# Token weights loaded in 9216-byte runs and turned as fp32 products with the identity, the first queries too

## The chip, the core and the metric

The kernel runs on one core of a Trainium2 chip. The metric is the device time of the program in microseconds (us). TensorE (PE) multiplies, VectorE (DVE), ScalarE (ACT) and GpSimd (POOL) do the rest, SyncE (SP) and ACT issue the transfers (DMA).

## The reference

Eight batches, eight heads, 576 tokens, head size 64, all fp32. Linear attention with a norm, then a block that mixes tokens and channels:

```python
kv  = einsum('bhsd,bhse->bhde', k, v)
out = einsum('bhsd,bhde->bhse', q, kv)
x   = out / sqrt(mean(out*out, -1) + 1e-6) * g_norm      # then heads side by side: (8, 576, 512)
theta = x @ w_theta
zr, zi = x * cos(theta), x * sin(theta)
u = x + einsum('ts,bsd->btd', w_tok_r, zr) + einsum('ts,bsd->btd', w_tok_i, zi)
result = u + maximum(u @ w_ch, 0)
```

The token weights w_tok_r and w_tok_i are 576 x 576. The mix contracts over s, so PE needs them with s on the partitions; in memory they lie with t as rows. They must be turned once.

## The kernel before

**Tiling.** The 576 tokens of a batch are cut into four tiles of 128 rows and one of 64 tokens, whose two halves of 256 columns share the 128 partitions (`full(j)` tells them apart). Token g*9 + r lies at place r*64 + g, so that a partition reads long runs from memory.

**A batch** is: kv (L262, fp32 products of 64 x 64 in four quarters of the array, two calls of 36), its copy to the block matrix kbd (L278), turning of q (L293, or by a transposing transfer from batch 2 on, L301), raw = q kv (L332), square and sum (L355, L365), the root on POOL (L371), x (L380), turn of x (L403), theta (L444), the sine and cosine (L449 to L491; abs, L468, is on ACT or DVE), z (L493, in zm and zt; on DVE or POOL), the token mix (L510), u (L528), turn of u (L536), channel mix (L546), gain (L551), the last sum (L561), store (L576).

**The first stage**, which the change touches: q, k and v of batch 0 and the weights come in by loads on the two queues of SP and ACT. The fp32 token weights land in the buffers that K and V of batch 1 use later (`wtok_s`, L201), the rows of the last 64 places in `wtail_s` (L202). Each matrix comes as two half loads of 64 partitions, in runs of 2304 bytes, and a tail (L229). `cast_token` (L236) makes fp16 of them in `wn` and `wnt`, ten casts on DVE, ACT and POOL. `w_turn` (L591) turns the casts with ten fp16 transposes for each of nine pieces (four and one for each half of the partitions), and `w_out` (L602) copies 576 columns to `wT`. The fp32 queries of batch 0 and all later ones land in `q_s`, which shares memory with `wn` (L204), are cast (L223) and turned (L293). `idle` (L605) runs products whose result nobody reads.

**The order** is written out by hand: the code after L611 makes a list of tasks with engine, cost and what each needs; `TURNS` (L35 to L98) gives the order in which the tasks are issued, the PSUM bank of each (`@3`) and the engine where it isn't the first choice (`:A`, `:D`, `:G`); `~28` is 28 idle products. The costs in the task list play no part when the kernel runs. Each engine works through its own instructions strictly in that order. Transfers share eight completion counters in turn: a load that reuses a counter is issued only when the load before it on that counter has landed. `tok_ready` (L692) holds the casts, `w_turns` (L752) the turns of the weights; K and V of batch 1 wait for the casts (L719, L721), q of batch 1 for all turns (L753).

Of the kernel before, what the change touches and what calls it, by code (L numbers as in the profile page):

```python
# [35 lines left out]
0 2 3 23 12 6 52 24 9 17 13 25 14 7 10 8 39 4 11 26:A 33 15:G 16:D 53 20 5 27:G 18 ~28@0 117@0 110@1  # L36
21 111:A 131@2 124@3 118:A 132:D 138@4 29 19 28 22 104@5 36 40 125:D 37 46 106:A 105 34 139 112@7
119@1 113 38 120 114 35 107@2 121 115 30 45:D 109:A 108:D 31 49 126@0 122 116 140@5 127 133@6 32 134
128 50 43:A 129 135 47 41:A 123 141 51 44:D 42 136 130 48 92 ~8@2 71@4 248 60 145@2 93 62:A 154@3
61:D 67@7 59:G 142 72:A 75@1 94 146:D 68:A 143 155:D 147@0 137 58:A 95 156@4 144 148 56 57 249 55  # L40
63@2 54 157 172@3 149 250 79@7 76:A 158 69@6 88 181@5 251 150 73@0 160 173:D 163@1 159:A 65@4 89
164:D 161 77@3 64 174@1 151 81 90 162 152 66:D 165@2 91 175 153 96 80:A 182:D 200@4 82 166:D 78 70
221@5 167 83 176 183@7 169 84 168 233@3 74 184:D 259@1 170 185 85 186 178 177 212@6 171 260 97 187
188 201 179 190 98 222 244 180 99 189 261 86 87:A 245 234 262 252 246 264@0 263:A 191@7 265 247
271@1 235 202 253 266@2 203 213 267 254 272:D 292@0 214 268 293 255 273@4 236 413@0 269 274 215 256
402 275 101 294@3 403 414 192 276 295 270 193 404 296 100:D 223 194 405 102:G 257:A 278@6 415 224
258 279 418 237@2 416 417:D 285@7 280@5 297 286 216@6 277 281 287@0 419 103:D 308@1 228 288 299@7
195@4 420 300:D 217 282 301@7 309 421 406 289 283 310@6 196:D 298 407 302:D 311 290 303 408 312 305
422@1 436@4 409 284 225@3 550 218@7 219 423 226:D 551 291 437 314 1 424 326@6 410 317@5 304:A 335@3
327:D 438 306 328@0 552 427 240 313 336 307 227@6 315 425 553 220 318 337@3 229 428 204@7 316 319@5  # L50
412 205 429 329:D 238 197@6 398 430 426 320 411 239@7 330 399 579 366@2 321 332 198 400 322 354@1
323 338:D 241 331:A 580 439 431@0 199 206@5 432 401 339 324 433 441@7 375@6 333 581 325 434 345@3
442 440 582 558 367 341 443 340:A 342 346 207 435 559 344 451@4 460@0 444 452 376 334 560 461 343
453@4 554 561 462@0 445 454 555 208 377 455 562 347 463:D 469@7 556 570 368 378 470 478@5 457 348
557 446@4 565@6 456:A 464 447 571 369 563 458 471@3 566 479:D 466 572 230 448 459 480@0 564 573 472
209 465:A 379@2 231 387@5 467 380:D 449 567 473 710 232 481 468 352 474:A 210 355 450 568 482 569
349@2 211 373 370@3 475 574@4 371:D 356 575 711 350:D 583@6 576 372@7 584 712 357 483:A 577 487@0
351@3 713 585 484 488 593@2 485 714 353 588@1 388 586 589 578 389 731 489@0 594 590 717@3 490 374
382 476 732 491 527@7 587 718 715:A 591 733 390 518@0 477 734 612@6 706 486 381@5 613 722 361 707
592 493 519 492:A 494 708 528 496 358@6 614@1 723 359:D 595 719 709 615 495 596 383 724 598@6 721  # L60
520 616 725 854 716 529 597 720 855 618 521 735@5 603@1 599 497@3 394 736 862 856 600 621@4 604 737
525 360@2 857 622:D 726@0 530 630@1 738 727 623@4 863 631:D 617:A 728 605@7 619 864 362 601 498
624:D 363 606 865 740@1 625 729 632@2 866 607 384 499 608 609 364 620:G 522@4 610 500 506@7 365
626:A 730 507 523 385 602 745@3 739 531@0 741 501@6 386 524@4 867 858 611 532 742 859 508 627 526
743 1024 628 670@5 860 509 633 764@0 649@4 765:D 746 861 634 639@7 502 534 533@0 640:D 636 744 1025
641@2 868 629 750@6 1026 539@7 751 642:D 540 635:A 747 541 1027 702 671 643 748 542 1033 703 645
1019@1 535 637 752 704 644:A 646 513 755@7 1020 766@0 647 756 1034 749 504 757@7 705 767 648 658@3
768 753 1035 1021 758:D 769:A 1036 638 510@0 759 883 1023 672 1022 760 773@7 511:D 761 1028@1 774:D
782@2 884 1029 650 673 770 1037@0 885 1030 503@7 762 754 1031 886 1038 659 505 771 874 1047@5 1039
660 1032 674@6 1040 651 875 661 1042@7 512@1 783:D 876 536 1043 763:G 1048 1041 869@2 877 1044 537  # L70
1012 652 775@0 870 772 538 1045 784@4 675:D 776 1013 1049 679@6 777 1014 1050 871 1046 778:A 1015
514 779 791@0 872 873:D 680 677 1016 780 1051 681 1008 785:D 1057 781:G 887@7 653@1 1009 682 888
878@2 676@3 879 786 1058 792 683@5 889 662@6 793@4 654:D 890 1010 801@0 794 663 795 822@1 1059 880
797 787:A 823 686 678 1011 1074 684 802 796:A 881 798 892@4 685@6 788 800 1075 789 799 810@3 893 656
1076 515 790 897@5 1017:A 811 687 812 546 882 516 1004 1067@6 894 898 1005 891 1060@2 1068 813 517
895 391@7 803 1069 1006 907 824 392:D 1071 1061:D 1052@3 665 1007 1070 691@6 899 692 693 1062 908
1077@7 900 694 1063:A 896 909 1084@2 1064 804 1072 1018 655@6 1159 825 1065 901 805@4 1053 1154@0
1073:G 1085 1066 1160 1078 1086 831@5 1161 1155 1079 1087:A 917@2 1162 1054 806:D 1081 1055 657 924
910@7 1080:A 1082 1156 911:D 1088 1083:G 925 1056 1089 918:D 902@4 393@6 926 1158 912 832 1157 919
903 1168 814@3 913:A 1090:G 1163@7 1110@0 1164 833 921 1165 1169 920:A 664@1 395 1170 1091 922 815:D  # L80
1166 904 934@2 914 834 1171 915 688 666 826@6 1177@3 1092 927@5 827 817 923 667 1167 689 1122@1 928
905 543@6 935 1123 929 690 544 808 1172@7 936 843@5 668 1173 1093@6 937:A 1174 844 669 930:A 845
1094:D 1175 807@2 1178 906 846 931 941 1179 835@4 1111 836 809 916:G 816@5 1176 942 1095 1131@4 1192
1096 1097 818 1182@2 1098 1101@7 1180 1099 938 1193 1102 1100 939 1132 1183 1194 829 1112 932 1103
1113 850 695@6 972@5 1184 1114 696 838 1104 1124 1181 951@0 1105 1115 1185 1125 828@6 933 819 1106
1133 830 940:G 837@7 1186 1126 820 952 821 396 545@3 1117 943@1 1127 547 1187@6 839 1202@2 1188 944
397 1134 1108 960@3 1209 945 1189 947 1107@7 698 946:A 948 1210 961 1190 950 981@4 1109 1211 1116@1
1191 1203:D 1226 847@7 973 1118 1195@6 949 1129 242 1227 1204 962 1196 1138 1135 953 243 1206 1197
1205:A 982 954 1198:A 840 1136 974 963 1207 983 975 1199 1208:G 841 1212@1 1200 976 842 848 1219@2
# [32 lines left out]
def kernel(  # L122
# [844 lines left out]
```

## Time and profile before

| what | value |
|---|---|
| median of 3 runs | 237.19 us (235.02 to 238.41) |
| the profiled execution's own time | 236.83 us |
| its span | 235.1 us |
| busy: PE, DVE, ACT, POOL | 208.4, 181.9, 127.3, 147.1 us |
| chain that ended last: PE, DVE, DMA | 33%, 31%, 15% |
| mean granted clock of TensorE | 0.951 |
| moved by DMA | 49.41 MB, mean 210 GB/s |

The page gives times from the start of the span. L12 is line 12 of the kernel. PE is TensorE at products, PEld its weight loads. A timeline row reads: start, busy time, engine, line, operation, out<-in, shape, count, and in brackets the idle time before it and what ended it. A row of the chain reads: start, length, engine or transfer, out (or line), count. An fp32 product written once in the code shows as two records.

### The profile page before, as it was taken

The page shows a single profiled execution, that of the slowest core. Times are in us where ns is not written, and L with a number is a line of the kernel's source. Part 1 is how long each engine was busy: PE and PEld are TensorE (multiplying, and loading weights), DVE is VectorE, ACT ScalarE, POOL GpSimd, SP SyncE. Part 2 cuts the span into 40 slices and gives each one's busy share as a digit, 9 for nine tenths or more (in the row PEclk, how much of TensorE's full clock was granted, in tenths as well). Part 3 has the DMA queues.
Part 4 walks back from the last instruction along what each step waited for, and adds up shares of the span by engine and source line. Part 5 has one row for each costly group of instructions (what it writes and reads, how often), then busy time and mean ns, then how long its engine had stood idle before and what let it go on. Part 6 is the DMA issues. An engine that isn't in the chain of part 4 may idle for free.

```text
span 235.1 us, 6095 instructions
## 1 busy us (share of the span) xinstructions
PE 208.4 (89%) x2488; PEld 119.7 (51%) x2488; DVE 181.9 (77%) x340; ACT 127.3 (54%) x242; POOL 147.1 (63%) x114
## 2 busy tenths in 40 slices
PE   7866799997779799999897999989799999999971
PEld 2355358564634356655453556545455454564530
DVE  1124755857699998989998989799989978699570
ACT  3033466854775759947485636846796512840100
POOL 3205920027699666769868099978599987566750
PEclk9965559999999999999999999999999999999997
DMA  5999897799798999758999997874543367755676
GB/s 177 347 246 279 190 344 266 219 368 355 179 231 259 360 348 280 95 196 301 287 216 151 211 255 191 263 216 84 98 110 84 65 143 85 165 138 104 168 188 146
DMA packets 47627, 49.41 MB, mean 210 GB/s; under 512 B 28016, under 2 KB 29040, under 8 KB 47600
## 3 DMA queue, kind: packets, MB, share of 16 engines
q1 hardware_dynamic: 38688, 29.53, 54.5%
q10 hardware_dynamic: 8912, 19.50, 25.6%
q8 instruction: 19, 0.31, 0.6%
q14 instruction: 8, 0.07, 0.2%
HBM read 33.10 MB, written 9.44 MB: 181 GB/s over the span
## 4 chain that ended last, share of the span: by engine, by line
PE 33%; DVE 31%; DMA 15%; ACT 9%; issue 4%; SPq 3%; POOL 1%; ACTq 0%; DVEq 0%; POOLq 0%
PE psum L434 10%; PE psum L520 8%; DMA vt<-in_moe_w_tok_i_dram 5%; DVE arg L462 5%; DMA vt<-in_v_dram 5%; PE psum L271 4%; DVE ot L570 4%; DMA kt<-in_k_dram 4%; DVE x L387 4%; PE psum L287 3%; DVE zt L505 3%; DVE zm L497 3%; DVE ss L368 3%; DVE arg L473 3%; PE psum L597 2%
## 5 line engine op out<-in xcount | busy, mean ns | idle before, releaser
L375 POOL TENSOR_TENSOR rt<-ss,mhalf 128x8 f32<-128x8 f32 (+1 forms) x40 | 62.2, 1562 | 43.1 <-DVE ss L368 43.1
L520 PE MATMUL psum<-zm,wT 128*128 128x512 f16 x256 | 67.0, 379 | 1.8 <-DVE zm L497 1.0
L554 POOL TENSOR_TENSOR ug<-u,g 128x512 f32<-128x512 f16 (+1 forms) x40 | 44.1, 1114 | 8.2 <-DVE ot L570 8.1
L520 PEld LDWEIGHTS <-wT 128*128 128x128 f16 x288 | 26.2, 98 | 31.0 <-issue 5.3
L434 PE MATMUL psum<-wth,xT 128*128 128x512 f16 x128 | 32.4, 392 | 2.0 <-DVE arg L462 1.3
L434 PE MATMUL psum<-wch,uT 128*128 128x512 f16 x128 | 32.5, 379 | 1.6 <-DVE uT L319 0.8
L481 ACT ACTIVATE sc<-arg 128x512 f16<-128x512 f32 (+1 forms) x40 | 23.1, 583 | 12.2 <-DVE arg L462 12.2
L570 DVE SCALAR_TENSOR_TENSOR ot<-psum,ug 128x512 f32<-128x512 f32 (+1 forms) x40 | 24.7, 631 | 6.5 <-PE psum L439 3.5
L488 ACT ACTIVATE sc<-arg,quarter 128x512 f16<-128x512 f32 (+1 forms) x40 | 26.6, 673 | 4.0 <-DVE arg L473 3.5
L462 DVE SCALAR_TENSOR_TENSOR arg<-pt,psum 128x512 f32<-128x512 f32 (+1 forms) x40 | 24.4, 626 | 4.8 <-ACT pt L453 4.6
L497 POOL TENSOR_TENSOR zm<-x,sc 128x1024 f16<-128x1024 f16 x11 | 23.8, 2175 | 6.3 <-ACT sc L488 6.3
L271 PE MATMUL psum<-vt,kt 64*64 64x64 f32 x1152 | 22.5, 232 | 5.7 <-DMA vt<-in_v_dram 3.0
L319 POOL CAST qh<-wn 128x1152 f16<-128x1152 f32 (+1 forms) x12 | 12.9, 1087 | 23.3 <-DMA wn<-in_q_dram 23.3
L531 DVE TENSOR_TENSOR u<-psum,x 128x512 f16<-128x512 f32 (+1 forms) x40 | 24.4, 628 | 3.5 <-PE psum L520 3.5
L271 PEld LDWEIGHTS psum<-vt,kt 64*64 64x64 f32 x1152 | 20.3, 145 | 10.1 <-issue 4.5
L368 DVE TENSOR_REDUCE ss<-sqb 128x8 f32<-128x520 f32 x32 | 21.8, 686 | 3.9 <-ACT sqb L359 3.6
L359 ACT ACTIVATE sqb<-psum 128x512 f32<-128x512 f32 x32 | 18.5, 593 | 9.5 <-PE psum L345 9.2
L387 DVE TENSOR_TENSOR x<-psum,rt 128x512 f16<-128x512 f32 x32 | 21.9, 683 | 1.0 <-POOL rt L375 0.9
L453 ACT ACTIVATE pt<-psum 128x512 f32<-128x512 f32 (+1 forms) x25 | 13.7, 560 | 15.9 <-PE psum L434 12.5
L434 PEld LDWEIGHTS <-xT 128*128 128x128 f16 x128 | 11.8, 100 | 16.2 <-issue 3.8
L497 DVE TENSOR_TENSOR zm<-x,sc 128x1024 f16<-128x1024 f16 x21 | 19.9, 951 | 0.1
L471 ACT ACTIVATE arg<-arg 128x512 f32<-128x512 f32 (+1 forms) x27 | 15.5, 581 | 7.0 <-DVE arg L462 7.0
(77 smaller groups left out, 271.3 us busy)
## 6 DMA issues: line engine op xcount, KB each, us to landing
vt<-in_v_dram ACTq DMA_DIRECT2D x7, 1152.0 KB, 7.1
kt<-in_k_dram ACTq DMA_DIRECT2D x7, 1152.0 KB, 6.2
wn<-in_q_dram SPq DMA_DIRECT2D x14, 576.0 KB, 6.8
out_dram<-ot SPq DMA_DIRECT2D x28, 256.0 KB, 3.6
kt<-in_k_dram SPq DMA_DIRECT2D x2, 576.0 KB, 9.9
vt<-in_v_dram ACTq DMA_DIRECT2D x2, 576.0 KB, 10.7
zm<-in_moe_w_theta_dram SPq DMA_DIRECT2D x1, 1024.0 KB, 15.8
zm<-in_moe_w_ch_dram SPq DMA_DIRECT2D x1, 1024.0 KB, 9.3
```

Source lines behind the costliest of these rows:

```text
L271: nc.tensor.matmul(kv_ps[b, lo][at:at + D, i, m - lo, :], kt[b % NKV][rows, hp, j * D:(j + 1) * D], vt[b % NKV][rows, hp, j * D:(j + 1) * ...
L368: nc.vector.reduce_sum(out=ss[:], in_=sq_sb.pop((b, j))[:], axis=AXX)
L375: nc.gpsimd.tensor_tensor(out=rt[:], in0=ss[:], in1=mhalf[:, 0:h], op=ALU.pow)
L387: nc.vector.tensor_tensor(out=x_pair[b, p][:, :, a * HC:(a + 1) * HC].rearrange("p t (h e) -> p t h e", e=D), in0=r[:].rearrange("p (t h e ...
L434: nc.tensor.matmul(t[:], lhs[:, kc, :], w[:, kc, :], start=first, stop=last)
L462: nc.vector.scalar_tensor_tensor(out=arg[:, 0, :], in0=pt_sb.pop((b, j))[:], scalar=MAGIC, in1=th_ps.pop((b, j))[:], op0=ALU.subtract, op1 ...
L488: nc.scalar.activation(out=sc_sb[b, j][:, 1, :], in_=arg_sb.pop((b, j))[:, 1, :], func=AFT.Sin, bias=quarter[:], scale=-TURN * SHRINK,)
L497: e.tensor_tensor(out=zm[b % NZ][:, j, :, :], in0=x.unsqueeze(1).broadcast_to((P, 2, C)), in1=sc[:], op=ALU.mult,)
L520: nc.tensor.matmul(t[:], wT[:, w, j * P:(j + 1) * P], r, start=first, stop=last)
L531: nc.vector.tensor_tensor(out=u[:], in0=y_ps.pop((b, j))[:], in1=x_sb.pop((b, j)), op=ALU.add)
L554: nc.gpsimd.tensor_tensor(out=ug[:].rearrange("p (h e) -> p h e", h=h), in0=u_sb[b, j][:].rearrange("p (h e) -> p h e", h=h), in1=g8[:].un ...
L570: nc.vector.scalar_tensor_tensor(out=ot, in0=v_ps.pop((b, j))[:], scalar=0.0, in1=ug_sb.pop((b, j))[:], op0=ALU.max, op1=ALU.add,)
```

## The change

- `load_token` is one load for each matrix, 128 partitions with one run of 9216 bytes each (w_tok_i on SP, w_tok_r on ACT); the tail is a load of its own. Partition 2g + o now holds rows 4o to 4o + 3 of group g.
- The casts of the token weights are gone, and `wn` and `wnt` with them. `turn_f` turns fp32 data by an ordinary product with an fp32 identity (`ident_f`, a new copy on DVE). `w_turn` does four such products for each half of the partitions, 128 columns each, written to PSUM in the order that `wT` needs; `w_out` copies 512 columns and casts. The tails are turned and copied by two tasks of their own.
- The queries of batch 0 aren't cast either: `q_turn` turns them from `q_s`, eight products of 128 columns a block, alternating between the two halves of the partitions. `q_s` has memory of its own.
- K and V of batch 1 wait for the turns of the weights; q of batch 1 waits only for the turned queries of batch 0.
- `TURNS` is new from end to end. On PE the first stage now has 38, 4, 4, 4, 3, 9 and 9 idle products (28 and 8 before), the first token pieces come in one block of three, the theta products come after all nine pieces. Over the whole program abs moves from ACT to DVE nine times, and zm from DVE to POOL four times, three of them in batch 0.

The diff, without `TURNS` and the costs of tasks:

```diff
@@ -179,13 +178,13 @@
-    wn = const.tile([P, NJ, 2 * S], FP16, name="wn")
-    wnt = const.tile([P, 2, S], FP16, name="wnt")
+    q_s = const.tile([P, NHP, TJ * D], FP32, name="q_s")
+    ident_f = const.tile([P, P], FP32, name="ident_f")
@@ -201,8 +200,6 @@
-    q_s = wn[:].rearrange("p j s -> p (j s)").bitcast(FP32).rearrange("p (n e) -> p n e", n=NHP)
     def load_pairs(eng, dst, src, b, ns):
@@ -226,19 +223,15 @@
-    def load_token(eng, i, o):
+    def load_token(eng, i):
-        if o < 2:
-            eng.dma_start(out=wtok_s[i][o * TL:(o + 1) * TL, :, :], in_=w_in[:, o:TJ - 1:2, :])
-        else:
-            eng.dma_start(out=wtail_s[:, i, :], in_=w_in[:, TJ - 1, :])
-    def cast_token(i, j):
-        if full(j):
-            dst, src = wn[:, j, i * S:(i + 1) * S], wtok_s[i][:, j, :]
-        else:
-            dst, src = wnt[0:TL, i, :], wtail_s[:, i, :]
-        copy_out(dst, src)
+        eng.dma_start(
+            out=wtok_s[i].rearrange("p j s -> p (j s)"),
+            in_=w_in[:, 0:TJ - 1, :].rearrange("g (o j) s -> g o (j s)", o=2))
+    def load_token_tail(eng, i):
+        w_in = (moe_w_tok_r, moe_w_tok_i)[i].rearrange("(g r) s -> g r s", r=TJ)
+        eng.dma_start(out=wtail_s[:, i, :], in_=w_in[:, TJ - 1, :])
     def scale_g():
@@ -290,7 +283,22 @@
+    def turn_f(dst, src, n=P):
+        rhs = ident_f[0:n, 0:n]
+        if len(dst.shape) == 3:
+            rhs = rhs.rearrange("p (g o) -> p g o", o=2)
+        nc.tensor.matmul(dst, src, rhs, start=True, stop=True)
     def q_turn(b, j):
+        if b == 0:
+            p, a = divmod(j, 2)
+            blocks = [(a, NJ * p + m) for m in range(HH)] if full(j) else [(m, TJ - 1) for m in range(2)]
+            t = bank(len(blocks) * P).rearrange("p (m e) -> p m e", e=P)
+            for m, (a, r) in enumerate(blocks):
+                for n in range(2):
+                    turn_f(t[n * D:(n + 1) * D, m, :], q_s[:, 2 * a + n, r * D:(r + 1) * D])
+            tr_ps["q", b, j] = t
+            return
@@ -588,19 +596,31 @@
     def prep(dst, src, kc, by):
+    def w_part(n, o):
+        return (1 - n % 2, n // 2 * 2 + o) if n < 2 * NJ else (o, TJ - 1)
     def w_turn(n):
-        t = psum[:, now[-1].bank, :].bitcast(FP16)[:, 0:NT * P]
+        t = bank()
-            rows = slice(o * TL, (o + 1) * TL)
-            i, r = (1 - n % 2, n // 2 * 2 + o) if n < 2 * NJ else (o, TJ - 1)
+            i, r = w_part(n, o)
+            to = t[o * TL:(o + 1) * TL, :].rearrange("p (o j g) -> p j g o", o=2, j=NJ)
-                nc.tensor.transpose(
-                    t[rows, jj * P:(jj + 1) * P], wn[:, jj, i * S + r:(i + 1) * S:TJ], ident[:])
-            nc.tensor.transpose(t[rows, SM:SM + P], wnt[:, i, r::TJ], ident[:])
+                turn_f(to[:, jj, :, :], wtok_s[i][:, jj, r::TJ])
     def w_out(n):
-        copy_out(wT[:, n, :], tr_ps.pop(("w", n))[:, 0:S])
+        copy_out(wT[:, n, 0:SM], tr_ps.pop(("w", n)))
+    def w_tail_turn(ns):
+        t = bank(len(ns) * TL).rearrange("p (n g) -> p n g", g=TL)
+        for n in ns:
+            for o in range(2):
+                i, r = w_part(n, o)
+                turn_f(t[o * TL:(o + 1) * TL, n - ns[0], :], wtail_s[:, i, r::TJ], TL)
+        tr_ps["wtail", ns[0]] = t
+    def w_tail_out(ns):
+        copy_out(wT[:, ns[0]:ns[-1] + 1, SM:], tr_ps.pop(("wtail", ns[0])))
     def idle(n):
@@ -678,9 +698,7 @@
     def load_q0(a):
-        q_got[0, a] = [add("qc", e, {"ACT": 0.63, "DVE": 0.66}[e],
-                           lambda n=n: cast_q(0, slice(n, n + 1)), [h], -45, alts=cast_alts(TJ * D))
-                       for n, e in ((2 * a, "DVE"), (2 * a + 1, "ACT"))]
+        q_got[0, a] = [h]
@@ -689,18 +707,14 @@
-    tok_ready = {0: [], 1: []}
+    tok_got, tail_got = {}, {}
-        h = []
-        for o, queue in enumerate(("SP", "ACT", "SP")):
-            eng = nc.sync if queue == "SP" else nc.scalar
-            h.append(load(queue, 0.62, 1.55 if o < 2 else 0.5, lambda i=i, o=o, eng=eng: load_token(eng, i, o),
-                          [sp if queue == "SP" else act], -42 - i + 0.1 * o,
-                          16 if o < 2 else 4, 2.8)[1])
-        for j, e in enumerate(("DVE", "ACT", "POOL", "ACT" if i else "DVE", "POOL")):
-            tok_ready[i].append(add("tc", e, {"DVE": 0.5, "ACT": 0.63, "POOL": 0.72}[e],
-                                    lambda i=i, j=j: cast_token(i, j), (h[0:2] if full(j) else h[2:]) + q_got[0, 0] + q_got[0, 1], -41,
-                                    alts=(("DVE", 0.5), ("ACT", 0.63), ("POOL", 0.72))))
+        queue = "SP" if i else "ACT"
+        eng = nc.sync if i else nc.scalar
+        hold = sp if i else act
+        tok_got[i] = load(queue, 0.5, 3.4, lambda i=i, eng=eng: load_token(eng, i), [hold], -42 - i, 32, 2.8)[1]
+        tail_got[i] = load(queue, 0.5, 0.5, lambda i=i, eng=eng: load_token_tail(eng, i), [hold], -41.5 - i, 4,
+                           2.8)[1]
     def load_next_q(b, was, pos):
@@ -717,11 +731,11 @@
-                         old + (tok_ready[0] if b == 1 else []), at - 0.5)
+                         old + (w_turns if b == 1 else []), at - 0.5)
-                         old + (tok_ready[1] if b == 1 else []), at)
+                         old + ([w_turns[n] for n in (0, 2, 4, 6, 8)] if b == 1 else []), at)
-            _, got["wch"] = load("SP", 0.5, 2.7, load_wch, [sp, *tok_ready[0]], -37, 32)
+            _, got["wch"] = load("SP", 0.5, 2.7, load_wch, [sp], -37, 32)
@@ -734,24 +748,28 @@
-    w_ready = []
-    def w_all():
-        turns = []
-        for n in range(2 * NJ + 1):
-            t1 = add("wt", "PE", 0.36, lambda n=n: w_turn(n),
-                     tok_ready[1] * (1 - n % 2) + tok_ready[0] * (n % 2 or n == 2 * NJ), n * 0.1, [PS], shape=1)
-            e = "ACT" if n % 2 else "DVE"
-            t2 = add("wo", e, 0.52 if e == "ACT" else 0.37, lambda n=n: w_out(n), [t1], n * 0.1,
-                     alts=(("DVE", 0.37) if e == "ACT" else ("ACT", 0.52),))
-            t1.readers = [t2]
-            w_ready.append(t2)
-            turns.append(t1)
-        return turns
-    w_turns = w_all()
-    load_next_q(1, w_turns, -36)
+    w_turns, w_ready, w_tails = [], [], []
+    for n in range(2 * NJ + 1):
+        t1 = add("wt", "PE", 0.55, lambda n=n: w_turn(n),
+                 [tok_got[i] for i in (0, 1) if n == 2 * NJ or i != n % 2], n * 0.1, [PS], shape=1)
+        e = "ACT" if n % 2 else "DVE"
+        t2 = add("wo", e, 0.52 if e == "ACT" else 0.6, lambda n=n: w_out(n), [t1], n * 0.1,
+                 alts=(("DVE", 0.6) if e == "ACT" else ("ACT", 0.52),))
+        t1.readers = [t2]
+        w_ready.append(t2)
+        w_turns.append(t1)
+    tail_outs = []
+    for ns in (list(range(2 * NJ)), [2 * NJ]):
+        t1 = add("wtl", "PE", 0.8 if len(ns) > 1 else 0.12, lambda ns=ns: w_tail_turn(ns),
+                 [tail_got[0], tail_got[1]], 1.0, [PS], shape=2)
+        t2 = add("wtlo", "ACT", 0.52 if len(ns) > 1 else 0.2, lambda ns=ns: w_tail_out(ns), [t1], 1.0,
+                 alts=(("DVE", 0.6 if len(ns) > 1 else 0.15),))
+        t1.readers = [t2]
+        tail_outs.append(t2)
+        w_tails.append(t1)
+        if b == 1:
+            load_next_q(1, all_of("qt", 0), -36)
...
@@ -856,7 +875,7 @@
-                        tok_ready[0] + tok_ready[1] if b == 0 else [])]
+                        w_tails if b == 0 else [])]
@@ -875,7 +894,7 @@
-                        [*z_ready[:(2, 3, NT + 1)[part]], *w_ready[:3 * part + 3], head, y],
+                        [*z_ready[:(2, 3, NT + 1)[part]], *w_ready[:3 * part + 3], *([] if full(j) else tail_outs), head, y],
@@ -923,13 +942,13 @@
+        nc.vector.tensor_copy(out=ident_f[:], in_=ident[:])
-        nc.gpsimd.memset(wnt[TL:P, :, :], 0.0)
```

More of the change, by code (lines that the diff above doesn't have):

```diff
@@ L86 @@
[L86 to L89, printed above, removed]
-1213 955 977 1214 1128@6 1201:G 1220 1215 1216 993@0 1221 964 956 1217 994 1222 697@3 1218 849@5
@@ L98 @@
+840 1267 1272@7 1243 1273 1274@1 1244 841 1276 1277 1245 1278
 """.split()
```

126 lines of the change are left out of this document (65 added, 61 removed).

## The prediction

> **What bounds the kernel now.** I read the page first: span, slices, then the chain that ended last, then the same chain for the first 62 us alone, then busy time by stretches, the timeline and the table of transfers. From the page:
>
> ```profile
> span 235.1 us, 6095 instructions
> ...
> PE   7866799997779799999897999989799999999971
> ...
> PEclk9965559999999999999999999999999999999997
> ```
>
> From about 60 us on PE is busy nine tenths and more, and PE and DVE share the chain (33% and 31%). The early slices are thinner and hold the only fall of the clock, to half, in slices 4 to 6. The change sits in this first stage. Its chain:
>
> ```profile
> 3.01 10.89 DMA vt<-in_v_dram
> 13.92 12.34 DMA vt<-in_moe_w_tok_i_dram
> 26.34 0.51 ACT wn L313
> ...
> 28.47 0.61 PE psum L597 x4
> ...
> 31.93 3.11 PE psum L434 x8
> 35.03 0.66 PE psum L597 x7
> ...
> 39.17 0.66 PE psum L597 x7
> ...
> 40.65 1.85 PE psum L434 x8
> ...
> 46.36 9.02 DMA kt<-in_k_dram
> ...
> 55.52 1.28 PE psum L271 x72
> ...
> 59.31 1.21 PE psum L271 x72
> ```
>
> Until 26.3 us the chain is transfers, then the casts of the token weights, then TensorE alone (turns of token weights at L597, theta at L434) to 42.5. The stretches agree (duration; PE, PEld, DVE, ACT, POOL busy; clock; DMA share; GB/s):
>
> ```profile
> 14.00:27.50 13.50, 10.31 (x172) 7.00 (x172) 6.79 (x17) 4.50 (x11) 6.68 (x5) 0.50 1.05 253
> 27.50:34.50 7.00, 6.40 (x45) 4.13 (x46) 4.09 (x10) 4.09 (x9) 3.30 (x3) 0.50 0.80 269
> 34.50:44.30 9.80, 9.80 (x99) 6.96 (x99) 6.27 (x13) 7.06 (x13) 0.00 (x0) 1.00 0.74 250
> ```
>
> From 34.5 to 44.3 PE has no gap at all: here product time added is time lost. Two lines of the timeline give the places of the first products:
>
> ```profile
> 1.44 9.02 PE L608 MATMUL psum<-fill,ident 128*128 128x512 f16 x28 [1.44 <-DVE fill L927]
> 11.25 1.17 PE L287 MATMUL psum<-ident,qh 128*128 128x128 f16 x18 [0.79 <-DVE qh L319]
> ```
>
> **The change, part by part.** The changed order (engine by engine, with what each instruction waits for) gives the places; durations come from the profiled execution, which took 236.83 us at a span of 235.10; the median of the runs is 237.19, 0.15% above, so the sum stands for both.
>
> *Casts removed.* Ten token casts (0.44 to 0.67 us each) and four query casts go. On the chain stand 26.34 to 28.47, so at most 2.1 us. ident_f costs DVE one small copy (0.2) ahead of the fill, so idle products start at 2.0, not 1.44.
>
> *Transfers.* The two token matrices now come as one load each instead of two half loads (10.1 to 17.8 us to landing each). SP issues its first seven loads without a wait, w_tok_i among them at about 4 us (before 10.52). Against that, each ACT load now waits for an SP load to land (they share completion counters): the second half of V(0) for the second half of K(0) (about 14.6, where before it was issued at 8.49), and w_tok_r for w_tok_i. Landing of w_tok_i: by 14.6 some 3.4 MB have come, at about 280 GB/s; 1.4 MB are left (its own 1.18 and a share of V) at 253 to 346 GB/s, 4.0 to 5.5 us, so 18.6 to 20.1; I take 19.5. PE needs it at 26.7: hidden. But ACT stands at the w_tok_r issue until then, and the copy of the first kv product, which PE needs for the first raw products, is queued behind it: 19.5 + 0.6 issue + 0.4 copy = 20.5 where PE would be ready at 19.9. Cost 0.6; 0 to 2 by the ends. V(0)'s second half: 14.7 plus 7.1 (V row) to 10.7 (half V row) is 21.8 to 25.4; PE wants it at 23: 0 to 2.4, I take 0, because fewer bytes are ahead of it in its queue. w_tok_r: 20.1 plus 7 to 10 is 27 to 30, wanted at 33: hidden.
>
> *Price of an fp32 product.* L271 runs 36 products of 64 columns on a quarter of the array each, four at a time: 1.21 us, so 0.134 each. fp16 products scale with columns (four of 512 take 0.86, eight of 128 take 0.45, 0.056 each). A turn here has 128 columns and half the array: 0.134 if columns don't count, 0.268 if they count fully; without L271's start 0.23, which I take. Two such products run side by side only when neighbours in the order lie in different halves. q_turn alternates halves: 4 x 0.23 = 0.9 a block. w_turn issues four in one half, then four in the other: 8 x 0.23 = 1.8 with no overlap (in the fp16 turns, two in the 1.48 us from 39.17 to 40.65, none shows), 0.54 if packed at 0.134, 1.5 if only the products at each change of half overlap. I take 1.5.
>
> The Trainium skill ("FP8 and Floating Point Precision", TensorE Precision Notes) says a true fp32 product takes four passes; as an estimate from that page, four times L287's 0.056 is 0.22, and a turn 1.45: the sum would be 0.4 us lower. It speaks against the cheap end, 0.134.
>
> *The ledger of PE.* Idle: 12 slow ones (0.43) to 7.2, where the clock came up before too, then 26 at 0.216: ends 12.8, so the queries are turned later than before (11.25). 16 pairs of query products 3.7: 16.5. Four idle 0.86, kv 1.2: 18.6. Query tail 0.5, four idle 0.86: 19.9, wait to 20.5. Eight raw 0.45, 18 token tails in 9 pairs at 0.134 1.2, four idle 0.86: 23.0. kv 1.2, three idle 0.65, eight raw 0.45, nine idle 1.95: 27.3. Then nine w_turns 13.5, 18 turns of x 1.0, raw 0.2, theta 4 x 0.87 + 0.61 = 4.1, eight query turns of batch 1 0.45, nine idle 1.95: 48.5 where the token mix starts. Before, PE has done theta at 44.2, and six mix products (1.3) too, but not the eight query turns (0.45): 43.4 for the same work. So PE comes 5.1 us late, though it gains the full clock (half clock cost the two kv 2.0 of 2.20 each against 1.21, and theta 1.3).
>
> *What takes over.* K(1) follows w_turns and theta on ACT's queue and moves as they do. In batch 0 three of four zm now go to POOL (2.2 each against DVE 0.68): the last ends near 55, wanted near 56; hidden, just. Before, PE stood 1.4 us for K(2) ahead of 55.52; PE comes later now, so this wait goes: -1.4. After that the work is the same and the slip of 3.7 stays to the end.
>
> *Later batches.* The whole order is written anew. DVE takes eight more abs of 0.78 us and one small one, and gives up four zm, three of them in batch 0: net some 5.6 us; DVE is 31% of the chain, so 1.7. ACT loses nine abs at 0.62; it is 9% of the chain, so -0.5. That is 1.2 if nothing hides it and 0 if all is hidden; I take 0.6. The order itself has no row; the nearest is the "issue" share of the chain, 4% of the 175 us after the first stage, 7 us, of which a new order may win or lose some 3.
>
> Sum: 236.83 + 5.1 - 1.4 + 0.6 = 241.1, said as 241.0.
>
> **The rivals.**
>
> *The products are cheap (the other side).* If w_turn costs 0.8 and a query pair 0.134, PE gains 9 x 0.7 + 18 x 0.1 = 8.1, of which some 0.6 to 1.4 is lost again in K(2)'s wait: about 234, and 231 at 0.54 a turn. For it: L271 may be paced by weights, not columns. Against: every fp16 row scales with columns. It decides below 1.04 us a turn (1.5 less 4.2/9): there the change turns into a gain. 20%.
>
> *The clock falls again.* Before, it fell near 14.2 after a stretch in which PE was busy 1.62 of 4 us. If it falls between 13 and 27 for half of that work, 6 to 7 us are added: 247. Against: the new order leaves no gap above 1 us there. 10%. The Trainium skill ("TensorE: Matmul & The Clock Gate", Part 4) says that transposes don't count as busy for the gate, while these are plain products; that would make the fall less likely; the row above, with turns alone at 11.25, agrees.
>
> *Transfers late.* V(0)'s second half at 25.4 or w_tok_i at 22: 2.4 or 2.0 on PE at once; if w_tok_r needs the 17.8 us of its slowest row, 38 instead of 33, 5 us. 243 to 246. 13%.
>
> *The rest of the order decides.* Loads and busy sums past 60 us hardly differ, but a plan with other costs may fit better or worse by 3 to 5 us: 236 or 245 as the two ends. 12%.
>
> **How the numbers follow.** The main case (turn 1.3 to 1.8, full clock) has 45% and gives 238 to 245, likeliest 241.0. What this kernel's measurement can tell from no change is about 2%: 232.4 and 241.9. Faster: 8 of the cheap case's 20 and 4 of the last's 12: 0.12. Within: 24 of the main 45, 12 cheap, 2 of late transfers, 5 of the last: 0.43. Slower: 21 main, 10 clock, 11 late, 3 last: 0.45. The range leaves out the cheapest products and the longest cold stretch: 232.5 to 246.5.
>
> **What would show it.** In the changed profile: L628's first 38 products end near 12.8; the eight-product turns at L290 in stretches of 1.3 to 1.8 us, nine of them between 27 and 46; granted clock 1.00 from 7 to 60; w_tok_i landed by 20; token mix (L528, L532) starting near 48 against 42.3; the kbd copy on ACT right behind the w_tok_r issue. It is wrong if a turn takes under 1.0 us, if the clock row shows a five, if PE waits for vt or kt before 40, or if the mix starts by 43 and the end still moves.

## The result, and the profile after

The changed kernel takes 245.47 us (median of 4 runs, 244.93 to 246.66), the kernel before 236.54 beside it on the same chip: ratio 1.038, 95% interval 1.029 to 1.047. It is slower by 3.8%, where 1.7% (241.0) had been forecast. The profiled execution took 244.93 us, its span is 243.1 (before 235.1), so 8.0 us of span have to be found; 4.3 had been forecast (5.1 - 1.4 + 0.6). In e7, e9, e11, e15 and e17 the median includes disturbed executions, which the ratio leaves out, so read the ratio there; in e7 and e17 it rests on two executions.

The page of the changed kernel, span, busy tenths of PE and granted clock:

```profile
span 243.1 us, 6433 instructions
...
PE   6989999988989897996999799999988999998970
...
PEclk9999999999999999999999999999999999999998
```

The hole of the early slices is gone (6 9 8 9 where 7 8 6 6 stood), and so is the fall of the clock. Still the span is longer: PE is busier with more work. The chain of the first 70 us (start, duration, what) shows with which:

```profile
2.74 7.79 DMA zm<-in_moe_w_tok_i_dram
10.55 8.81 DMA g<-in_g_norm_dram
...
20.34 0.30 DVE kbd L327
...
20.69 0.61 PE psum L353 x8
21.30 2.32 PE psum L290 x36
23.62 0.97 PE psum L628 x4
24.59 1.21 PE psum L264 x72
...
27.11 1.94 PE psum L628 x9
29.05 3.74 PE psum L290 x45
...
36.15 1.75 PE psum L290 x16
...
38.23 4.26 PE psum L290 x48
42.49 1.83 PE psum L442 x8
...
48.73 1.17 DVE wch L329
49.90 0.60 DVE wT L327
50.50 0.60 DVE zm L505
51.10 0.52 DVE arg L481
...
53.30 1.58 DVE arg L481
...
57.11 1.01 DVE zt L513
...
62.55 1.21 PE psum L264 x72
...
66.26 0.66 PE psum L264 x33
66.92 1.10 issue
68.02 0.81 PE psum L264 x39
```

Two things are to be seen. From 20.69 to 44.33 the chain is TensorE without a break, and the token turns (L290, 16 records are the 8 products of a turn, since each fp32 product leaves two) fill 29.05 to 42.49. From 44.48 on the chain does not stay on TensorE: to 59.94 it runs over VectorE's instructions (11.7 of 15.5 us), with 2.6 us of ACT between them. Before, a transfer of K (46.36, 9.02 us) stood there. The second half of the key-value product of that stretch ended at 60.5 before; now it ends at 68.8, 8.3 us later. The two orders differ, but behind these two points TensorE has nearly the same work left (busy 156.9 us before, 156.2 now). Not all of the 8.3 is lateness from what stood ahead: this half began only 7.0 us later than before (66.26, before 59.31), and 1.10 us is a pause inside it for which the profile names no releaser. Before, such a pause stood 0.8 us behind the same product:

```profile
61.29 0.90 issue
```

With the pauses left out on both sides the lateness is 7.0 us, with both counted 7.4. So nearly the whole loss is there by 69 us.

The stretches say the same (length; PE, PEld, DVE, ACT, POOL busy; clock; DMA share; GB/s):

```profile
27.11:42.50 15.39, 15.39 (x166) 13.64 (x165) 8.33 (x15) 4.21 (x8) 6.54 (x6) 1.00 0.46 159
42.50:50.10 7.60, 7.30 (x51) 3.61 (x52) 5.62 (x12) 6.10 (x12) 2.61 (x2) 1.00 0.87 319
50.10:69.00 18.90, 15.94 (x369) 10.04 (x369) 14.72 (x26) 8.36 (x16) 13.37 (x9) 1.00 0.95 250
```

In the first PE is busy for every one of 15.39 us at full clock; in the last it has 3 us of gaps while VectorE does 14.72 of 18.90. At the end the lateness is still there: VectorE's last result (`ot`, L578) is done 6.2 us later than before (236.54, before 230.32), and a row of stores on SP, 0.6 us each and issued back to back, adds 1.8 us behind it.

### The profile page after: what moved, and what is told of

The parts are those of the page before. It is cut to its first block, busy times and chain, and to the rows that moved or that the text cites. A ratio compares the mean times of both kernels' runs of the same rounds, so it can differ in the third digit from the quotient of the medians.

```text
span 243.1 us, 6433 instructions
## 1 busy us (share of the span) xinstructions
PE 218.7 (90%) x2667; PEld 130.0 (53%) x2667; DVE 190.0 (78%) x347; ACT 117.4 (48%) x224; POOL 150.8 (62%) x113
## 4 chain that ended last, share of the span: by engine, by line
PE 49%; DVE 32%; DMA 7%; issue 4%; ACT 3%; POOL 1%; SPq 1%; DVEq 0%; ACTq 0%; POOLq 0%
PE psum L528 14%; PE psum L442 14%; DVE zt L513 6%; PE psum L290 6%; DVE arg L470 4%; DMA g<-in_g_norm_dram 4%; DVE arg L481 3%; DMA zm<-in_moe_w_tok_i_dram 3%; PE psum L264 3%; DVE zm L505 3%; PE psum L280 3%; DVE u L539 3%; DVE ot L578 3%; PE psum L353 3%; DVE ss L376 3%
## 5 line engine op out<-in xcount | busy, mean ns | idle before, releaser
L562 POOL TENSOR_TENSOR ug<-u,g 128x512 f32<-128x512 f16 (+1 forms) x40 | 43.3, 1094 | 21.2 <-DVE ot L578 16.6
L505 POOL TENSOR_TENSOR zm<-x,sc 128x1024 f16<-128x1024 f16 x15 | 32.9, 2195 | 11.8 <-ACT sc L496 11.8
L442 PE MATMUL psum<-wch,uT 128*128 128x512 f16 x128 | 32.7, 379 | 0.8 <-DVE uT L327 0.5
L442 PE MATMUL psum<-wth,xT 128*128 128x512 f16 x128 | 31.9, 379 | 0.7 <-DVE arg L470 0.3
L578 DVE SCALAR_TENSOR_TENSOR ot<-psum,ug 128x512 f32<-128x512 f32 (+1 forms) x40 | 25.0, 631 | 3.9 <-PE psum L442 1.7
L264 PE MATMUL psum<-vt,kt 64*64 64x64 f32 x1152 | 20.9, 221 | 3.3 <-DVE uT L327 1.6
L264 PEld LDWEIGHTS psum<-vt,kt 64*64 64x64 f32 x1152 | 18.6, 135 | 8.7 <-issue 4.9
L513 DVE TENSOR_TENSOR zt<-x,sc 64x256 f16<-64x256 f16 x32 | 20.4, 638 | 2.8 <-ACT sc L496 2.5
L628 PE MATMUL psum<-fill,ident 128*128 128x512 f16 x71 | 18.0, 404 | 2.1 <-DVE fill L947 2.1
L442 PEld LDWEIGHTS <-uT 128*128 128x128 f16 x128 | 11.7, 98 | 13.5 <-issue 1.6
L442 PEld LDWEIGHTS <-xT 128*128 128x128 f16 x128 | 11.7, 98 | 13.1 <-issue 1.0
L461 ACT ACTIVATE pt<-psum 128x512 f32<-128x512 f32 (+1 forms) x27 | 14.4, 542 | 5.7 <-PE psum L442 5.6
```

Source lines behind the costliest of these rows:

```text
L264: nc.tensor.matmul(kv_ps[b, lo][at:at + D, i, m - lo, :], kt[b % NKV][rows, hp, j * D:(j + 1) * D], vt[b % NKV][rows, hp, j * D:(j + 1) * ...
L442: nc.tensor.matmul(t[:], lhs[:, kc, :], w[:, kc, :], start=first, stop=last)
L505: e.tensor_tensor(out=zm[b % NZ][:, j, :, :], in0=x.unsqueeze(1).broadcast_to((P, 2, C)), in1=sc[:], op=ALU.mult,)
L513: e.tensor_tensor(out=zt[b % NZ][lo:lo + TL, hh * HC:(hh + 1) * HC], in0=x[rows, :], in1=sc[rows, i, :], op=ALU.mult,)
L562: nc.gpsimd.tensor_tensor(out=ug[:].rearrange("p (h e) -> p h e", h=h), in0=u_sb[b, j][:].rearrange("p (h e) -> p h e", h=h), in1=g8[:].un ...
L578: nc.vector.scalar_tensor_tensor(out=ot, in0=v_ps.pop((b, j))[:], scalar=0.0, in1=ug_sb.pop((b, j))[:], op0=ALU.max, op1=ALU.add,)
```

## The experiments

Theory A: what counts is TensorE's time up to the first mixing, because of the fp32 products. Theory D, the rival that grew out of the chain above: behind it VectorE sets the pace, with work that the new order moved onto it. Ratios are against the kernel before in the same call (its median there 235.5 to 236.4 us); the interval is 95%. A step of under about one point from one row to another lies inside the intervals.

| run | edit | us | ratio | interval |
|---|---|---|---|---|
| e1 | token turns by turns on the halves | 243.58 | 1.030 | 1.020 to 1.040 |
| e2 | without the six later idle groups | 243.47 | 1.032 | 1.024 to 1.040 |
| e3 | load of the norm's weights first | 246.44 | 1.044 | 1.036 to 1.052 |
| e4 | start's products read as fp16 | 239.78 | 1.015 | 1.006 to 1.025 |
| e5 | absolute values on their old engines | 242.92 | 1.029 | 1.021 to 1.037 |
| e6 | e5 and the x products too | 245.37 | 1.042 | 1.033 to 1.051 |
| e7 | all kinds on their old engines | 250.95 | 1.053 | 1.040 to 1.066 |
| e8 | e6 with e1 and e2 | 244.58 | 1.034 | 1.027 to 1.041 |
| e9 | e5 with e1 and e2 | 240.63 | 1.014 | 1.009 to 1.020 |
| e11 | e1, e2, all absolute values on ACT | 237.31 | 0.998 | 0.993 to 1.003 |
| e12 | kernel before, absolute values as after | 236.32 | 1.000 | 0.996 to 1.004 |
| e14 | e5 again | 243.70 | 1.029 | 1.022 to 1.036 |
| e15 | e4 with e5 | 235.49 | 0.996 | 0.992 to 1.001 |
| e16 | kernel before, all absolute values on ACT | 233.40 | 0.985 | 0.977 to 0.993 |
| e17 | all absolute values on ACT | 242.36 | 1.012 | 1.001 to 1.022 |
| e18 | kernel before with 26 more idle products | 241.07 | 1.017 | 1.009 to 1.024 |

### The order of the halves (e1)

```diff
-        for o in range(2):
-            i, r = w_part(n, o)
-            to = t[o * TL:(o + 1) * TL, :].rearrange(...)
-            for jj in range(NJ):
+        for jj in range(NJ):
+            for o in range(2):
+                i, r = w_part(n, o)
+                to = t[o * TL:(o + 1) * TL, :].rearrange(...)
                 turn_f(to[:, jj, :, :], wtok_s[i][:, jj, r::TJ])
```

> The eight fp32 products of a token turn write the upper and the lower half of PSUM by turns (o inside jj) instead of four and four. Theory A (PE's time up to the first mixing sets the end, and only neighbours of opposite halves overlap, as in the first queries' pairs at 0.23 us a pair): a turn falls from 1.42 us to about 0.92, nine turns by 4.3 us (13.45 us for the stretch to about 9.2), and the time falls by about 4, from 245.5 to 241.5. Theory B (after 42 us VectorE's row of arg, abs, wch and wT copies and the load of K(1) set the pace): the stretch falls alike, but the first mixing moves by under 1.5 us and the time by 0 to 1.5. Theory C (such products cost the same in any order): no change.

The turns got cheaper, and then something else took over. The chain of e1 from its first turn on:

```profile
30.28 3.13 PE psum L290 x43
...
35.84 1.19 PE psum L290 x16
...
37.75 2.40 DVE wth L329 x2
...
40.80 1.24 PE psum L442 x5
```

The 16 records that took 1.75 us take 1.19; over all nine turns the mean falls from 1.40 to 1.07 us. So products of opposite halves do overlap, though not to the 0.92 that theory A named. Theta (L442) now waits for VectorE's copies of its weights, two of which take 2.40 us; the wait itself is 0.32 us. Theta starts at 40.80 in place of 42.49. The turns themselves began 1.2 us later in this run, behind a later load of queries, so the edit brought 2.9 us to theta. The ratio fell by 0.8 points, about 2 us, inside the intervals and nearer to B than to A. In the trace 1.4 us of the gain are still there at 105 us; it is lost at the two later places that e2 shows, and VectorE's last result comes 0.8 us later. (e1's profiled execution took 245.16 us, its median is 243.58.)

### The idle products (e2)

The groups `~4@0`, `~4@0`, `~4@1`, `~3@1`, `~9@3` and `~9@1` are taken out of the order.

> Only the first 38 idle products stay; the six later groups (4, 4, 4, 3, 9 and 9, 33 products, about 7 us by 0.215 us each) are left out. Theory A (idle products are time of PE that the path pays, and the clock holds with fp32 products alone): the first mixing comes up to 5 us sooner (some of the 7 only fills waits for V(0) and the raw products) and the time falls by 3 to 5, to 240.5 to 242.5. Theory B (without them the granted clock falls to half in the token turns, as it was between 14 and 34 us in the kernel before): the nine turns cost up to twice, 13 us more, and the time is 250 to 256. Theory C (another engine sets the pace after 42 us): within 1.5 of 245.5.

The first mixing came 2.6 us sooner, yet from 135 to 183 us VectorE's instructions stand where they stood, to 0.02 us. The gain was given back at three places. At the first mixing TensorE, without the nine idle products ahead of it, stands 2.95 us for VectorE's zm, and the clock falls to half from 49.5 to 52.9 us; 0.4 us are lost. The second place is another fall of the clock. The changed kernel and then e2, at the same products:

```profile
115.47 1.89 PE L528 MATMUL psum<-zm,wT 128*128 128x512 f16 x8 [2.42 <-DVE x L395]
```

```profile
113.27 2.57 PE L528 MATMUL psum<-zm,wT 128*128 128x512 f16 x8 [2.42 <-DVE x L395]
```

The stretch 115:120 of the changed kernel and then of e2:

```profile
115.00:120.00 5.00, 4.53 (x33) 2.55 (x33) 4.93 (x10) 3.32 (x6) 2.32 (x2) 1.00 0.54 176
```

```profile
115.00:120.00 5.00, 5.00 (x30) 2.90 (x29) 3.45 (x7) 2.71 (x5) 4.01 (x3) 0.73 0.76 241
```

TensorE's pause ahead of these products is the same 2.42 us in both, but in e2 the clock falls to half behind it for 3.4 us, and 1.2 us are lost. It falls there in e1 and e3 too, and not in e4, behind a pause of 2.43 us in each; what decides is not shown. The third place is at 128 us, where an absolute value that took VectorE 0.41 us takes 2.38, and 1.0 us more is lost on balance; more on that below. What is left, 1.6 us of span, is at the end: VectorE's last result comes 0.2 us sooner, and the stores behind it take 1.3 us less. Theory A's 3 to 5 us did not come, and 0.6 points of ratio lie inside the intervals. Theory B did not come: the token turns kept the full clock without the idle products.

### The load of the norm's weights (e3)

```diff
-0 2 3 21 12 6 34 22 9 15 13 23 14 7 10 8 29 41 11 4 ~38@0
+0 2 3 21 12 4 6 34 22 9 15 13 23 14 7 10 8 29 41 11 ~38@0
```

> The load of the norm's weights is issued on ACT third, ahead of the first values and queries, instead of last at 10.55 us. It then lands by about 10 instead of 19.4, so VectorE's row of sums for it no longer stands before the copy that the first raw products wait for. Theory A: the first raw products start at 19.3 to 19.6 instead of 20.7 and the time falls by about 1. Theory B: the next product batch waits for the second half of V(0), which lands about 22, and the gain is lost there: no change (within 0.5). Theory C: the first values and queries land later by ACT's 0.6 us of issue, and the time rises by 0.5.

The sums for the norm were done by 18.1 us, but the first values were the price: ACT's next load now waited for a transfer of K. The chain of e3:

```profile
10.81 8.60 DMA vt<-in_v_dram
...
19.46 1.28 PE psum L264 x72
```

The first key-value product starts at 19.46 instead of 17.67, and the raw products 1.4 us later than in the changed kernel. 246.44 is 0.6 points over the changed kernel, inside the intervals: no gain, and C's sign with a larger price than C named.

### The price of fp32 (e4)

```diff
-        rhs = ident_f[0:n, 0:n]
+        rhs = ident[0:n, 0:n]
-                turn_f(to[:, jj, :, :], wtok_s[i][:, jj, r::TJ])
+                turn_f(to[:, jj, :, :], wtok_s[i].bitcast(FP16)[:, jj, 2 * r + 1::2 * TJ])
```

(The same for the first queries and the tails.)

> Price of fp32: the same products with the same tiles, counts, order and waits, but reading the upper two bytes of each fp32 word as an fp16 number with the fp16 identity. The values turned are then not the weights and not the queries; everything else is computed as before. Theory A: a token turn falls from 1.42 us to about 0.6 to 0.7 (8 products at 0.08), the stretch of the turns from 13.45 to about 6, the queries' turns from 4.1 to about 2.6 and the tails from 2.3 to about 1.2; the first mixing comes 8 to 10 us sooner, and the time falls to 236 to 239 (what lies behind, VectorE's row and the load of K(1), takes back some). Theory B (VectorE and K(1) set the pace after 42 us): the time falls by at most 2, to 243.5.

From e4's chain:

```profile
28.79 1.70 PE psum L290 x24
...
31.96 0.73 PE psum L290 x8
...
37.32 9.23 DMA kt<-in_k_dram
...
46.68 1.85 PE psum L264 x72
```

A turn (here 8 records, one for each product) costs 0.73 us where the same one took 1.75; over all nine the mean is 0.60 against 1.40. VectorE reaches its first arguments 6.9 us sooner. Then the load of K decides, as it did before the change, the clock falls to half from 47.2 to 50.6 us, and VectorE's last result comes 4.9 us sooner (4.6 of span). 1.038 falls to 1.015: the fp32 price is 2.3 points, 5.4 us, clear of the intervals, and nearer to theory A (239 at most) than to B. But the kernel is still slower than before, by 1.5%, with turns that cost no more than before (0.74, the two from 39.17 to 40.65).

### VectorE's later work (e5, e6, e7, e8, e14)

The new order also changed which engine does what behind the start: 22 of 40 absolute values on VectorE (13 before), 15 of 40 products with sine and cosine on POOL (11 before). Edits here are only letters in the order's table, as in `140` to `140:A`.

> Only the engines of the 40 absolute values go back to what they were in the kernel before (13 on VectorE, 27 on ACT, against 22 and 18 in the changed kernel); order, banks and all else stay. Theory D (behind the first theta product VectorE is what sets the pace, busy 209.9 us of 243.1 against 201.4 of 235.1, and part of the rise is these nine instructions, 14.6 us in place of 9.0): VectorE's work falls by about 5.6 us and the time by 2 to 4, to 241.5 to 243.5. Theory A (only the start's TensorE time counts): no change, 244.5 to 246.5. Theory E (ACT, with nine instructions of about 0.55 us more, holds up VectorE's arguments): 246 or more.

> The price run (products of the start read the upper halves of the fp32 words as fp16, so the weights and the first queries have other values) with the absolute values on their engines of the kernel before. Theory AD: the two gains, 4.6 and 3.3 us of span, add up, and what is left over the kernel before is nothing: 235 to 238. If a third cost is hidden in the new order: 239 or more.

(The kernel of e14 held only the second of the two edits named, so it is e5 once more; the pair was run as e15.) Nine absolute values on ACT instead of VectorE bring 1.0 and 0.9 points, 2.2 us, the low end of theory D. Each step alone lies inside the intervals; that A's "no change" falls is shown by e15 below, where the same nine bring 1.9 points, clear of them.

> As the run above, and the 40 products x by sine and cosine go back to their engines too (POOL 11 in place of 15). Theory D with collisions (VectorE's copies of fp16 products, L513, rose from 0.47 to 0.64 us and its absolute values stretch to 2.4 us where POOL's 2.2 us products run beside them): VectorE gets four products of 0.6 to 0.95 us, but fewer long meetings; its sum is 202 to 206 and the time 240 to 243. Theory D without collisions: VectorE's sum is 3 us above the run above and the time by 1 to 3 above it. Theory A: no change.

> All kinds behind the start that both kernels have (absolute values, products, copies of transposed x and u, whole turns, casts of queries) on their engines of the kernel before, in the changed kernel's order. Theory D: VectorE's sum comes to 201 to 204 as in the kernel before, and what stays over 236.3 is the slip of the start: 239 to 242. Theory A: no change. Theory E (an order made for other engines): 246 or more, since the copies stand in the wrong places on ACT and VectorE.

> Absolute values and products on their engines of the kernel before, with the six later groups of idle products left out and the token turns' products by turns on the two halves. If the start's TensorE time and VectorE's later work are both paid on one path (A with D), the gains add up: 2.6 us and 2 us at the first mixing, 2 to 4 behind it: 237 to 240. If VectorE alone sets the end (D), it is no better than the run with those engines alone by more than 1 us.

Theory D misses in all three. With the products back on VectorE the gain is gone (1.042), though the durations of VectorE's instructions add up to 201.4 us as in the kernel before (209.9 in the changed one); with all kinds back it is no better (1.053), in the range of theory E, whose reason would be that the order fits its own engines. So VectorE's sum alone is not the measure. What matters is where its long instructions fall, and the traces show why some are long. Copies for the short block (L513), the two that follow each other at 93.75, and POOL's product (L505) in the changed kernel:

```profile
92.84 0.29 DVE L513 TENSOR_TENSOR zt<-x,sc 64x256 f16<-64x256 f16 x1
...
93.75 2.49 DVE L513 TENSOR_TENSOR zt<-x,sc 64x256 f16<-64x256 f16 x2
```

```profile
93.68 2.12 POOL L505 TENSOR_TENSOR zm<-x,sc 128x1024 f16<-128x1024 f16 x1 [2.64 <-ACT sc L496]
```

One takes 0.29 us alone. The first of the two at 93.75 started 0.07 us behind POOL's product and ended 0.14 us behind its end: it had taken 2.18. Over the kernel (min, median, max in ns), after and then before:

```profile
L513 DVE TENSOR_TENSOR zt<-x,sc x32: 273/289/2228, 57.1 to 222.4; 64x256 f16<-64x256 f16 x32
```

```profile
L505 DVE TENSOR_TENSOR zt<-x,sc x32: 272/288/1286, 47.1 to 214.6; 64x256 f16<-64x256 f16 x32
```

Same median, longer tail. Summed over absolute values and both kinds of product, what lies over the duration alone (0.42, 0.29, 0.69) is 15.2 us before and 20.2 after. Every one of these that is over by more than 0.15 us runs beside an instruction of POOL that began first (a product, a gain, a copy or a cast), and ends 0.14 to 0.55 us behind its end. Behind POOL's products alone, 15 in place of 11, stand 9.5 us after and 5.1 before, which is 4.4 of the rise of 5.0. The Trainium skill ("SBUF — State Buffer", Who interferes with whom) says that VectorE and GpSimd share one pair of ports as an exclusive lock, so that the later of the two blocks for the whole instruction of the earlier; the rows above agree, 2.18 us against 0.29.

### All together (e9, e11, e17)

> The three edits that gained alone, together: absolute values on their engines of the kernel before (3.3 us of span), the token turns' products by turns on the halves (1.6 us at the first mixing), the six later groups of idle products left out (2.6 us at the first mixing). Theory AD (start and VectorE's later work lie on one path, and a gain at the start is given back only where VectorE meets POOL or TensorE's clock dips after an idle stretch): 236.5 to 239.5. If gains of the start are always given back behind 110 us: no better than 242 to 243 of the absolute values alone.

> As the run above, but all 40 absolute values on ACT. Theory D: VectorE loses 13 more instructions (8.5 us of its sum, 3.2 of it spent in meetings with POOL), and the time falls by another 1 to 3, to 235 to 238. Theory E (ACT sits between VectorE's argument and its product, and another 0.55 us on that way delays the products): 239 or more.

> The changed kernel with all 40 absolute values on ACT, nothing else changed. The run with the three edits gave 237.3 where the same with 13 left on VectorE gave 240.6; the same step from 243.3 gives 239.5 to 241. If only a start without idle products and with paired turns lets it through: 243 or more.

Start and later work do lie on one path: 1.032, 1.030 and 1.029 alone give 1.014 together, and with all absolute values on ACT the changed kernel draws level with the one before (0.998). e17, the same without the two edits of the start, is at 1.012. Its interval reaches that of e5, so the clear step is the one from e9 to e11. ACT had the room; theory E does not hold for it.

### The same edits in the old order (e12, e16, e18)

> The kernel before, with nothing changed but the engines of the 40 absolute values, which are those of the changed kernel (22 on VectorE in place of 13). No fp32 products, no other order. Theory D (part of the slowdown is VectorE's later work and has nothing to do with the turned weights): slower by 2 to 4, 238 to 240. Theory A (VectorE has room, the slip is all from the start): 235.5 to 237.

Theory D misses here: nine more absolute values on VectorE cost the old order nothing (1.000). These nine are dear only in the new order.

> The kernel before with all 40 absolute values on ACT, nothing else changed. If VectorE's later work bounds both orders alike: 2 to 4 us faster than the kernel before (232 to 234.5). If the old order has room on VectorE, as nine more absolute values on it cost nothing there: 235.5 to 237.5.

233.40 us, 1.5% faster than the kernel before, the best of all. The other 13 absolute values thus cost VectorE's row in both orders, and about the same: 1.7 points from e5 to e17, 1.6 from e9 to e11. With the best engines tried on each side, the changed kernel still loses: e11 over e16 is 0.998 / 0.985, 1.3%. The two were not measured side by side, and their intervals touch (0.993 to 1.003, 0.977 to 0.993).

```diff
-... 126:A 80:A 182:D 200@4 82 ...
+... 126:A 80:A 182:D ~26@4 200@4 82 ...
```

> The kernel before with 26 more idle products directly ahead of the first mixing product (26 by 0.216 us, 5.6 us of TensorE, in the bank that the mixing then takes). If a late start is carried to the end whole: slower by 5 to 6, 241.5 to 242.5. If loads and VectorE's waits absorb part, as the prediction had it: 240 to 241. If VectorE's and POOL's meetings make it more: 243 or more.

The extra products take what they should, in e18's chain:

```profile
42.74 1.83 PE psum L434 x8
44.57 5.61 PE psum L608 x26
50.18 1.29 PE psum L520 x6
```

In the profiled execution the mixing starts 7.9 us late (50.18 against 42.3; theta was 2.1 late already, which is not the edit's: the clock stayed at half until 36.2 us, before until 34.5), the key-value product that waited for K(2) before is 6.0 late, with no wait for the transfer any more, and from 75 us to the end VectorE's instructions stay between 5.5 and 5.1 late. So in the old order some 2 us are absorbed, most of it by that wait, and the rest goes to the end whole. Over the runs, 1.7%, 4.0 us for 5.6, which makes 240.4. The middle theory, the prediction's, holds here.

### Nothing else hidden (e15)

> The start's products read the upper halves of the fp32 words as fp16 (weights and first queries have other values), and the absolute values stand on their engines of the kernel before. If the two costs add up (ratios 1.0381 to 1.0152 and to 1.0285 alone): 1.005 to 1.01, 237.5 to 239. If the absolute values only help when the start is late: as with the products alone, 239 to 241. If a third cost is hidden: 240 or more.

0.996: with fp16 products and the nine absolute values moved, the whole 3.8% is gone. That is below every range named, 0.9 points more than the two gains added (2.3 and 1.0 points): the nine absolute values bring 1.9 points on top of e4. No third cost is needed.

## Why the prediction was off

Direction right, size off: 4.3 us of span forecast, 8.0 measured. Term by term, the 5.1 of TensorE's ledger came out as 7.75, the -1.4 of "what takes over" as +0.55, and the 0.6 of the later batches as -0.3. The first two failed, 4.6 us together by 69 us; the third gave 0.9 back.

- **The price of a product: right.** 1.5 us a turn taken, 1.42 measured (4.26 for three; 1.40 over all nine), and the reason holds in the main: neighbours in one half cost more than neighbours in opposite halves (1.40 and 1.07 a turn, e1), though the latter overlap only in part. The same products in fp16 take 0.60 a turn (e4). Each weight load of a token turn, which reads every ninth column, takes 0.21 us, that of the first queries, which reads columns in a row, 0.14; what this is worth was not tried. Clock at 1.00, right. The rival of cheap products falls twice: they are not cheap, and where they are (e4) the kernel is still slower, so its turning point of 1.04 us a turn was wrong as well.
- **The ledger of PE: a step that failed, mis-sized by 2.65 us.** Mixing at 51.15, not 48.5. The tails were priced in pairs, 1.2 us, and took 2.32 (0.129 for each of 18 products, no overlap seen); for that above all the turns began at 29.05, not 27.3, and as they were cheaper than put, they ended 0.5 late. Theta and the queries' turns, with some turns of x that had been put ahead of them, took 5.5 us (42.49 to 48.0) where 4.55 were put, and the mixing stood 1.0 us for VectorE's zm, a wait that the ledger did not have.
- **The wait at 20.5: right in time, wrong in cause.** The raw products started at 20.69, but ACT issued w_tok_r at 17 already, not at 19.5; the copy ahead of them stood on VectorE behind the sums of the norm's weights, whose load ACT had issued at 10.55 and which took 8.81 us to land. Taking that away gained nothing (e3).
- **"What takes over": the other step that failed, by 1.95 us.** It said that zm on POOL is "hidden, just", that PE's wait for K(2) goes, "-1.4", and that "after that the work is the same". e18 shows that a late TensorE alone does get that rebate, 1.9 us up to that product. In the changed kernel only half of it came: from 44.48 to 59.94 VectorE's row set the pace, with wT copies from fp32 PSUM (0.68 us; six of nine on VectorE, two of them in this stretch, where two of 0.45 stood before), a wch copy at 1.17, and absolute values and zt stretched to 1.58 and 1.01 beside POOL. The lateness of 7.75 us at the mixing (51.15 against 43.4 for the same work) was 7.0 at that product and, with the pause of 1.10 us inside it, 8.3 at its end, where 3.7 had been put. What the pause is stays open.
- **Later batches: the size not settled.** 0.6 was taken for the moved work. -0.3 shows behind 69 us (8.3 there, 8.0 at the end), or 0.6 to 1.0 if the pauses are counted alike on both sides, and 1.8 of the 8.0 are stores. Nine absolute values alone are worth 2.2 us in the new order (e5, e14), and more on top of e4. In e5's trace none of that gain is there by 69 us; VectorE's last result comes 1.5 us sooner. So the new order also won something back, and which part of it did was not tried.
- **"The rest of the order decides"** had 12%, and 245 as its bad end, which is where the time lies; e12 against e5 shows the mechanism: the same engine letters cost 0 in one order and 2.2 us in the other. That the total falls so near this rival's end is in part luck: 2.3 of the 3.8 points are the fp32 products' (e4), which it leaves out.

What stays open: how much of the later loss is the lock between VectorE and POOL and how much VectorE's plain load. e6 has the shorter meetings (13.0 us over, in place of 20.2) and did not gain.

## What to carry to other kernels

When a change moves work off one engine at the start, follow the path past the point where it joins the old one and sum up the next engine there too: here a transfer's wait that would have absorbed lateness had been replaced by a chain of fifteen microseconds, twelve of them VectorE's. A newly written order is a change of its own; compare which engine does each kind of work before and after, and price the instructions that can meet on a shared resource at their meeting price and not at their mean. To save a cast by an fp32 product pays only if the product's extra time, here 0.7 us a turn, is hidden, and neighbours should go to opposite halves of the array (1.07 us a turn in place of 1.40).

## What the runs showed that was not expected

An instruction of VectorE of 0.29 us takes 2.18 when it starts 0.07 us behind POOL's 2.12 us product. Where it falls is a matter of tenths: shifts of 1 to 3 us at the start (e1, e2) come out at the end as +0.8 and -0.2 on VectorE's last instructions. The same pause of TensorE, 2.42 to 2.43 us at the same products, was followed by half the clock for 3.4 us in three of five traces (e1, e2, e3) and by none of it in two (the changed kernel, e4). And of the idle products put in to hold the clock, 33 could go without a fall of it in the token turns; one came behind them, from 49.5 to 52.9 us.
